# Two interleaved memory-attention layers with gated feed-forward: weights fetched piece by piece, clearing moved to the prologue, one flip and two copies placed elsewhere

## The chip, the cores and the metric

The kernel runs on one core of a Trainium2 chip. Its time is device microseconds of one execution. Five engines work side by side: TensorE (PE in the profile; PEld is its weight load), VectorE (DVE), ScalarE (ACT), GpSimd (POOL) and SyncE (SP), which here issues nearly all DMAs. Each runs its own instructions in a fixed order and waits on semaphores for the others. Matmuls write to PSUM, whose eight banks VectorE or ScalarE must copy out ("evacuate") before they are used again.

## The reference

The input x has 2048 tokens of 448 elements. Two layers follow each other; each adds a memory attention and a gated feed-forward, and both layers use the same weights:

```python
x = x + attention(layernorm(x), mem0, Wq, Wk, Wv, Wo)
x = x + ((gate * (gate > 0)) * up) @ W_down     # gate, up from layernorm(x)
# attention, for 64 segments of 32 tokens, one after the other:
h = concat([mem, xs])                 # 8 memory rows and 32 tokens
scores = (h Wq)(h Wk)^T * scale       # 16 heads of 256; memory rows see
p = softmax(masked scores)            #   everything, tokens see backwards
o = (p (h Wv)) Wo                     # summed over the heads
mem = o[:8]; out = o[8:]
```

A segment needs the memory rows that the one before it left, so the 64 segments of a layer are a chain.

## The kernel before, in words

**Prologue** (L222 to L372). For each of eight pairs of heads the kernel loads Wq and Wk, turns them on TensorE and multiplies them into one matrix A_sb (with A3 and A3z for the last 64 rows of the 448); then Wv and Wo become B_sb. A segment then needs only h A, the scores, the weighted sum of h, and the product with B_sb. The products leave PSUM on VectorE and ScalarE. GpSimd sets up ident, the masks and the token buffers hT, and later clears TQ and xa (L341); after that it is idle until the loop begins.

**The loop** is `step(g, ff)` for g from 0 to 68, written out in full. Chain 0 is layer 1 on segment g, chain 1 is layer 2 on segment g - 4. Steps 4 to 63 have both chains (80 columns: two times 32 tokens and 8 memory rows); steps 0 to 3 and 64 to 67 have one (40 columns). In odd steps from the third on, a `Feed` object does the feed-forward of 128 rows in the gaps. The 16 heads are two halves (`hf`) of 28 tiles of 128 rows. A step goes:

- `pairs`, `wide`, `leave_bank`, `close_bank`: h A for the tiles of each half, into PSUM banks named b0 to b3 and z0 for half 0, c0 to c3 and z1 for half 1 (`prj` in the profile). `leave_bank` copies a bank into TQ, or TZ for the last 64 dimensions, the queries of that half.
- `scores_m`, `scores_x`: scores of the memory rows (`Sm`) and the tokens (`Sx`), then the softmax over VectorE (maximum mx, difference se, sum ssum, reciprocal rs, product) and ScalarE (exponential), into PM and PX.
- `flipped`, `flipped_rows`: PM or PX turned on TensorE into `pps` and copied out as PT.
- `weigh_m`, `weigh_m_rows`, `weigh_x`: the weighted sums of hk (the turned h). `weigh_m` makes two PSUM tiles, ya (tiles 0 to 15, 256 columns) and yb (tiles 16 to 27, 192 columns), and copies them into the memory columns of Y or Z (L711, L716). Y and Z are two buffers per half, 28 tiles x 80 columns, used in turns from step to step; token columns are filled by `weigh_x` a step ahead.
- `project_out`, `project_tail`: Y or Z times B_sb into `ox` (the first 384 output dimensions) and `o` (the last 64), over columns lo to hi; `finish` writes the new memory rows into hT for the next step and the outputs into OT. In step 0 the only outputs are eight memory columns, 32 to 40.

**Order.** On TensorE it is the order of the source: each matmul or turn is tied to the one before it (`in_order`, L73). On the other engines a scheduler orders the instructions by when it expects them to be ready, so the copy of one score can stand ahead of another that the source names first. A few are pinned (`keep_in_program_order`).

**Buffers.** The pool `glob` lasts for the whole kernel. The prologue's pool `pre` is closed at its end, and the pool `main` then takes its memory, so what is written first in `main` waits for the last use of `pre`. In `main` lie the feed-forward weights Wgu_sb and Wd_sb, and Y, Z, TZ, PX, PM, OT, hk and hh, which are cleared there (L404 to L419), Y, Z and hh by GpSimd, the others by VectorE; GpSimd also copies eight blocks of ident into TZ (L408).

**Feed-forward weights.** `load_ff(part)` (L381) issues up and gate rows (two DMAs of 224 KB) for parts 0 to 6, and 256 rows of Wd (one DMA) for parts 7 to 13. `load_some` issues two parts: at three places in steps 0 and 1, at two in step 2. Each DMA waits for the TensorE instruction that stands last in the source at that place.

Of the kernel before, what the change touches and what calls it, by code (L numbers as in the profile page):

```python
# [8 lines left out]
BF = mybir.dt.bfloat16  # L9
# [11 lines left out]
SEG = 32  # L21
L = MEM + SEG
F = 1792
FT = 14
# [6 lines left out]
NT = 28  # L31
HI = 128
HW = 5 * HI
W = 2 * L
XO = (0, 2 * L - SEG)
M0 = SEG
HX = (0, 64 + MEM)
HM = (SEG, 64)
QR = (64, 96)
NPASS = 7  # L40
ROWS = (slice(0, 64), slice(64, 128))


def chunk_of(i, r):

    return 6 if i == 3 else 2 * i + r if i < 3 else 2 * (i - 4) + 1 - r
# [7 lines left out]
def build_kernel(ctx, tc, A_x, A_mem0, A_Wq, A_Wk, A_Wv, A_Wo, B_W_gate, B_W_up, B_W_down, out,  # L54
                 ntiles=16, nseg=64):
    nc = tc.nc
    P = nc.NUM_PARTITIONS
# [9 lines left out]
    glob = ctx.enter_context(tc.tile_pool(name="glob", bufs=1))  # L67
# [19 lines left out]
    def behind_pe(r):  # L87
        tc.add_manual_dep(r.ins, last_pe[0],
                          mybir.DependencyInfo(mybir.DependencyClass.Sync, mybir.DependencyReason.DATA),
                          reason="order of work")  # L90
# [7 lines left out]
    xa = [glob.tile([P, DM], BF, name=f"xa{i}") for i in range(3)]  # L98
# [7 lines left out]
    ident = glob.tile([P, P], BF, name="ident")  # L106
# [49 lines left out]
    TQ = []  # L156
    for hf in range(2):
        t = glob.tile([P, 5, 6, 64], BF, name=f"TQ{hf}")
        TQ.append(t)

    def flip_banks():

# [59 lines left out]
    with tc.tile_pool(name="pre", bufs=3) as pre:  # L222
# [115 lines left out]
        idle(32)  # L338
        cur = flip_next(0)
        idle(16)  # L340
        for t in TQ + xa:  # L341
            behind_pe(nc.gpsimd.memset(t[:], 0.0))
        for p in range(NP):
            if p > 1:
                nxt = flip_next(p + 1)
            for _ in fuse_qk_parts(p, cur):
                if p < 2:
                    nxt = flip_next(p + 1)
            cur = nxt
            if p == 2:  # L350
                xn0 = normed(st0)
            if p == 4:
                tps0 = transpose_tokens(xn0)
                for b in range(2):
                    rows_in(nc.vector, b, 0, tps0[:, :, block(b)])
                mtp = psum.tile([P, 4, MEM], BF, tag="ps", name="mtp")
                for kd in range(4):
                    tr(mtp[:, kd, :], mem0_n[:, kd * 128:(kd + 1) * 128], ident[0:MEM, 0:MEM])
                nc.vector.tensor_copy(mem0T[:], mtp[:])
                set_mem(0, mem0T[:].unsqueeze(2), (0,))  # L360
# [17 lines left out]
    Wgu_sb = main.tile([P, NPASS, F], BF, name="Wgu_sb")  # L378
    Wd_sb = main.tile([P, FT, DM], BF, name="Wd_sb")

    def load_ff(part):  # L381

        def piece(dst, src):
            d = nc.sync.dma_start(dst, src)
            tc.add_manual_dep(d.ins, last_pe[0],
                              mybir.DependencyInfo(mybir.DependencyClass.Sync, mybir.DependencyReason.DATA),
                              reason="order of transfers")

        if part < NPASS:
            for r, src in enumerate((B_W_up, B_W_gate)):  # L390
                c = chunk_of(part, r)
                piece(Wgu_sb[ROWS[r], part, :], src[64 * c:64 * c + 64])
        else:
            f = slice(2 * (part - NPASS), 2 * (part - NPASS) + 2)
            piece(Wd_sb[:, f, :], B_W_down[f.start * P:f.stop * P].rearrange("(f p) d -> p f d", p=P))

    TZ, PX, PM = [], [], []
    YY = [[], []]
    swap = main.tile([P, W], F32, name="swap")
    for hf in range(2):  # L400
        for name, shape, where in (("Y", [P, NT, W], YY[hf]), ("Z", [P, NT, W], YY[hf]), ("TZ", [P, 5, 128], TZ),
                                   ("PX", [P, 4, 64], PX), ("PM", [P, 2, 64], PM)):
            t = main.tile(shape, BF, name=f"{name}{hf}")
            (nc.gpsimd if name in "YZ" else nc.vector).memset(t[:], 0.0)  # L404
            where.append(t)
        for part, q in enumerate(QR):
            for c in range(2):
                nc.gpsimd.tensor_copy(TZ[hf][q:q + 16, 3 * c + part, :].rearrange("p (h q) -> p h q", q=16),  # L408
                                      ident[q:q + 16, q:q + 16].unsqueeze(1).to_broadcast([16, 8, 16]))
    OT = main.tile([P, 4, 128], BF, name="OT")  # L410
    nc.vector.memset(OT[:], 0.0)
    xT = main.tile([P, NPASS, 128], BF, name="xT")
    hh = main.tile([P, FT, 128], BF, name="hh")
    part = main.tile([P, 2, DM], F32, name="part")
    nc.gpsimd.memset(hh[:], 0.0)
    HK = []
    for i in range(2):
        t = main.tile([P, 6, 128], BF, name=f"hk{i}")
        nc.vector.memset(t[:], 0.0)  # L419
        HK.append(t)  # L420


    class Feed:
# [133 lines left out]
    def wide(bk, chains, hb, j, tiles=slice(0, 6)):  # L557

        n = L * len(chains)
        for t in bk.tiles[tiles]:  # L560
            for kd in range(3):
                mm(bk.out(t, n), A_sb[:, kd, bk.hf, t, :], moving(hb, j, kd, chains),
                   start=(bk.empty and kd == 0 and t == bk.tiles[0]), stop=(not bk.empty and kd == 2),
                   skip_group_check=True)
        bk.empty = False
# [28 lines left out]
    def close_bank(bk, chains, hb, j, eng, **how):  # L594

        wide(bk, chains, hb, j)
        leave_bank(bk, chains, eng, **how)
# [49 lines left out]
    def active(g):  # L647
        return [c for c in (0, 1) if 0 <= g - c * LAG < nseg]

    at = [0]  # L650

    def step(g, ff):
        chains = active(g)
        xs = active(g - 1)
# [2 lines left out]
        hb = hTb[gb % 2]  # L657
        cols = [(0, 32) if c == 0 else (48, 80) for c in xs] + [(32, 40) if c == 0 else (40, 48) for c in ms]
        lo, hi = min(a for a, _ in cols), max(b for _, b in cols)
        last = g == nseg + LAG - 1  # L660
        now = 0 if chains else 1
        if not chains:
# [8 lines left out]
        def ys(hf, later=0):  # L671
            return YY[hf][(g + later) % 2]

# [28 lines left out]
        def probs_x(hf, Sp):  # L702
            weights_of(Sp, 4, PX[hf], f"x{hf}")

        def weigh_m(hf, hk, PT):
            if not ms:
                return
            ya = psum.tile([P, 256], F32, tag="ps", name="ya")
            for kd in range(2):
                mm(ya[:, kd * 128:kd * 128 + 128], hk[:, kd, :], PT[:], start=True, stop=True)  # L710
            nc.vector.tensor_copy(ys(hf)[:, 0:16, M0:M0 + 16], ya[:].rearrange("p (t q) -> p t q", q=16))  # L711
            yb = psum.tile([P, 192], F32, tag="ps", name="yb")
            mm(yb[:, 0:128], hk[:, 2, :], PT[:], start=True, stop=True)
            for eo in range(2):
                mm(yb[:, 128:192], hk[:, 4 + eo, :], PT[:, 64 * eo:64 * eo + 64], start=(eo == 0), stop=(eo == 1))
            nc.scalar.copy(ys(hf)[:, 16:28, M0:M0 + 16], yb[:].rearrange("p (t q) -> p t q", q=16))  # L716

        def weigh_m_rows(hf, hk, PT):
            pt = PT[:, 0:128].rearrange("p (t c m) -> p t c m", c=2, m=MEM)
# [49 lines left out]
        def project_out(hf, t0, t1):  # L769

            nonlocal ox
            if ox is None:
                ox = psum.tile([P, 3, W], F32, tag="ox", bufs=1, name="ox")
            for t in range(t0, t1):
                for mc in range(3):
                    mm(ox[:, mc, lo:hi], B_sb[:, hf, t, mc * 128:(mc + 1) * 128],
                       ys(hf, now)[:, t, lo:hi], start=(hf == 0 and t == 0 and mc == 0),
                       stop=(hf == 1 and t == NT - 1 and mc == 2), skip_group_check=True)
# [31 lines left out]
                for u in us:  # L810
                    ff.gate_up(u)

        def load_some():
            if g < 3:
                for part in (2 * at[0], 2 * at[0] + 1):
                    if part < NPASS + FT // 2:
                        load_ff(part)
                at[0] += 1

        if not chains:  # L820
            project_tail()
            project_out(0, 0, NT)
# [1 line left out]
            finish()  # L824
            return

        load_some()
        nc.gpsimd.tensor_copy(hb[ROWS[0], j, 4 * HI:4 * HI + 104], hb[ROWS[0], j, 3 * HI:3 * HI + 104])
        b0, b2 = Bank(0, 0), Bank(0, 2)
        pairs((b0, b2), chains, hb, j)  # L830
# [7 lines left out]
            ff.residual()  # L838
            ff.norm(nc.gpsimd if len(chains) == 2 else None)
        hk = hk_make(kps)  # L840
        load_some()
        b1, z0 = Bank(0, 1), Bank(0, 4)
        wide(b1, chains, hb, j)
        wide(z0, chains, hb, j)
# [6 lines left out]
        pairs((c0, c2, c1, c3), chains, hb, j)  # L851
        close_bank(b3, chains, hb, j, nc.vector, parts=(slice(2, 3), slice(0, 2), slice(3, 5)))
        close_bank(z1, chains, hb, j, nc.scalar)
        wide(c0, chains, hb, j, slice(0, 1))
        scores_m(0)
        wide(c0, chains, hb, j, slice(1, 6))
# [2 lines left out]
        close_bank(c1, chains, hb, j, nc.scalar if len(chains) == 2 else nc.vector)  # L859
        if ff is not None and len(chains) == 1:  # L860
            tps = ff.xposed()
        if len(chains) == 2:
            pm = flipped(PM[0], 1, "m0", own)
        close_bank(c3, chains, hb, j, nc.scalar, parts=(slice(0, 3), slice(3, 5)))
        if ff is not None and len(chains) == 1:
            ff.xposed_rest(tps)
        if len(chains) == 2:
# [14 lines left out]
        if last:  # L882
# [9 lines left out]
            ff.down()  # L892
            ff.leave()
            return
        if g < 2:
            load_some()
        if ff is not None:
            project_out(0, 0, 10)
            half1 = weights_begin(Sx1, 4, PX[1], "x1")
# [18 lines left out]
            weigh_x(1, hk, px1)  # L918
            return
        project_out(0, 0, 23)  # L920
        probs_x(1, Sx1)
        pm = flipped(PM[1], 1, "m1")
        px0 = flipped(PX[0], 2, "x0")
# [1 line left out]
        weigh_m_rows(1, hk, pm)  # L925
        weigh_x(0, hk, px0)
        project_tail()
        project_out(1, 0, 16)
        px1 = flipped(PX[1], 2, "x1")
        project_out(1, 16, NT)  # L930
        finish()
# [84 lines left out]
```

## Time and profile before

| | |
|---|---|
| median of three runs | 1559.07 us (1558.81 to 1559.97) |
| profiled execution, its own time | 1563.11 us |
| its span in the profile | 1561.2 us |
| PE busy | 1534.6 us (98%) |
| DVE, ACT, POOL busy | 1062.3, 805.3, 167.6 us |
| chain that ended last | PE 94%, DVE 3%, ACT 1%, issue 1%, POOL 1%, DMA 1% |
| prologue ends, step 0 begins on PE | 71.4 us |
| steps 1, 2, 3 begin on PE | 90.0, 106.8, 122.8 us |
| an even and an odd two-chain step | 17.7 and 26.4 us |

A line of a timeline gives start, duration, engine, source line, operation, output <- inputs, shape and count; neighbours of one kind are merged into one line, and in brackets stand the idle time before and what ended it. A line of the waits names who waited for whom, the microseconds in total, how often, and the longest. "issue" is a wait for nothing that the profile shows. PE's rows can be busy while its instructions are slow: the granted clock stands apart.

### The profile page before, as it was taken

Reading aid. Unit: us, or ns where it says so; the run is one execution under the profiler, and the core shown is the slowest. Engines: PE = TensorE matmul, PEld = TensorE weight load, DVE = VectorE, ACT = ScalarE, POOL = GpSimd, SP = SyncE. Lnnn points to the kernel's source line nnn. Section 1 sums busy time; section 2 is a strip of 40 time slices with the busy share of each in tenths; the row PEclk is TensorE's granted clock in tenths of the full one; section 3 lists DMA queues with packets and bytes.
Section 4 is the critical chain, followed back from the end, with each engine's and each line's share of the span. In section 5 each row is a group of like instructions: output and inputs, shape, how many; then the busy total and the mean of one; then the engine's idle time right before and its main releaser. Section 6 shows DMA issues by size and latency. Waiting matters only on the chain.

```text
span 1561.2 us, 97869 instructions
## 1 busy us (share of the span) xinstructions
PE 1534.6 (98%) x44947; PEld 1416.4 (91%) x44947; DVE 1062.3 (68%) x3810; ACT 805.3 (52%) x2378; POOL 167.6 (11%) x303
## 2 busy tenths in 40 slices
PE   9889999999999999999999999999999999999998
PEld 7588999999999999999999999999999999999987
DVE  6756766766667666666666667766676767667664
ACT  6634555555455545555455455554555455554443
POOL 3110111011001110111011110110011110110100
PEclk9989999999999999999999999999999999999998
DMA  9530000000000000000000000000000000000000
GB/s 280 144 96 9 9 10 8 6 9 10 10 10 10 10 10 5 9 10 10 10 10 10 10 8 6 10 10 10 10 10 10 10 7 7 10 9 7 7 7 6
DMA packets 29467, 33.10 MB, mean 21 GB/s; under 512 B 3320, under 2 KB 28160, under 8 KB 29056
## 3 DMA queue, kind: packets, MB, share of 16 engines
q1 hardware_dynamic: 28848, 26.74, 6.4%
q8 instruction: 351, 5.75, 1.5%
q14 instruction: 60, 0.49, 0.1%
q10 hardware_dynamic: 144, 0.11, 0.1%
q0 software_dynamic: 64, 0.01, 0.0%
HBM read 23.18 MB, written 1.84 MB: 16 GB/s over the span
## 4 chain that ended last, share of the span: by engine, by line
PE 94%; DVE 3%; ACT 1%; issue 1%; POOL 1%; DMA 1%; SPq 0%; POOLq 0%; ACTq 0%; DVEq 0%
PE prj L82 29%; PE ox L82 25%; PE ups L82 10%; PE dps L82 6%; PE o L82 5%; PE y L82 4%; PE Sx L82 3%; PE pps L85 1%; PE aps L82 1%; PE Sm L82 1%; PE bps L82 1%; PE tps L85 1%; PE gps L82 1%; PE flip L85 1%; PE tpw L85 1%
## 5 line engine op out<-in xcount | busy, mean ns | idle before, releaser
L82 PEld LDWEIGHTS <-B_sb 128*128 128x128 bf16 (+1 forms) x15232 | 492.7, 103 | 26.3 <-issue 18.2
L82 PE MATMUL prj<-hT,A_sb 128*128 128x80 bf16 (+1 forms) x11424 | 436.7, 200 | 0.9 <-issue 0.9
L82 PEld LDWEIGHTS <-A_sb 128*128 128x128 bf16 x11424 | 411.3, 100 | 8.6 <-issue 1.0
L82 PE MATMUL ox<-Y,B_sb 128*128 128x80 bf16 (+3 forms) x5712 | 218.5, 199 | 0.6 <-DVE Y L711 0.6
L82 PE MATMUL ox<-Z,B_sb 128*128 128x80 bf16 (+2 forms) x5712 | 218.3, 200 | 0.6 <-DVE Z L711 0.6
L82 PE MATMUL ups<-xT,Wgu_sb 64*128 64x128 bf16 (+1 forms) x3332 | 190.3, 213 | 2.1 <-DVE hh L469 1.3
L82 PE MATMUL gps<-xT,Wgu_sb 64*128 64x128 bf16 (+1 forms) x3332 | 190.1, 213 | 0.4 <-DVE Z L95 0.4
L94 ACT CAST TQ<-prj 128x480 bf16<-128x480 f32 (+3 forms) x424 | 176.2, 461 | 25.1 <-PE prj L82 22.6
L82 PEld LDWEIGHTS <-Wgu_sb 64*128 64x128 bf16 x6664 | 178.5, 94 | 5.3 <-issue 3.1
L95 DVE CAST TQ<-prj 128x192 bf16<-128x192 f32 (+3 forms) x364 | 139.2, 418 | 63.1 <-PE prj L82 63.1
L94 ACT CAST Z<-y 64x128 bf16<-64x128 f32 (+2 forms) x260 | 89.5, 371 | 141.9 <-PE y L82 85.7
L94 ACT CAST TZ<-prj 64x320 bf16<-64x320 f32 (+2 forms) x304 | 111.8, 378 | 79.6 <-PE prj L82 74.8
L468 ACT CAST ut<-ups 128x256 bf16<-128x256 f32 (+1 forms) x238 | 85.2, 359 | 79.1 <-PE gps L82 59.8
L469 DVE SCALAR_TENSOR_TENSOR hh<-gps,ut 128x256 bf16<-128x256 f32 (+1 forms) x238 | 94.0, 406 | 47.0 <-ACT ut L468 34.2
L94 ACT CAST Y<-y 128x512 bf16<-128x512 f32 (+1 forms) x252 | 87.5, 375 | 62.0 <-DVE Y L95 58.8
L94 ACT COPY hT<-tps 128x256 bf16<-128x256 bf16 x32 | 11.9, 372 | 192.6 <-DVE hT L95 192.6
L95 DVE CAST Z<-y 64x128 bf16<-64x128 f32 (+2 forms) x260 | 103.6, 420 | 9.0 <-ACT Z L94 4.6
L95 DVE CAST Y<-y 128x512 bf16<-128x512 f32 (+1 forms) x252 | 102.6, 418 | 9.0 <-ACT Y L94 3.7
L611 ACT ACTIVATE se<-se 128x80 f32<-128x80 f32 (+1 forms) x270 | 71.5, 298 | 48.2 <-DVE se L610 46.7
L617 DVE TENSOR_REDUCE ssum<-se 128x2 f32<-128x80 f32 (+1 forms) x270 | 70.4, 275 | 37.6 <-ACT se L611 36.8
L82 PE MATMUL dps<-Wd_sb,hh 128*128 128x448 bf16 (+1 forms) x476 | 92.0, 360 | 0.0
L180 POOL TENSOR_SCALAR rstd<-mv 128x1 f32<-128x1 f32 x67 | 15.2, 226 | 715.5 <-DVE mv L178 715.4
(133 smaller groups left out, 2227.2 us busy)
## 6 DMA issues: line engine op xcount, KB each, us to landing
wo<-in_A_Wo_dram SPq DMA_DIRECT2D x8, 448.0 KB, 6.1
nat<-in_A_Wq_dram SPq DMA_DIRECT2D x8, 384.0 KB, 6.1
nat<-in_A_Wk_dram SPq DMA_DIRECT2D x8, 384.0 KB, 6.1
nat<-in_A_Wv_dram SPq DMA_DIRECT2D x8, 384.0 KB, 6.7
xa<-in_A_x_dram SPq DMA_DIRECT2D x32, 56.0 KB, 2.3
xa<-xp SPq DMA_DIRECT2D x32, 56.0 KB, 1.9
out_dram<-xa SPq DMA_DIRECT2D x32, 56.0 KB, 2.0
xp<-in_A_x_dram SPq DMA_DIRECT2D x30, 56.0 KB, 2.2
```

The source lines that it names most:

```text
L82: in_order(nc.tensor.matmul(*a, **k))
L85: in_order(nc.tensor.transpose(*a))
L94: return nc.scalar.copy(dst, src)
L95: return eng.tensor_copy(dst, src)
L180: nc.gpsimd.tensor_scalar(out=rstd[:], in0=mv[:, 1:2], scalar1=EPS, scalar2=None, op0=ALU.add)
L468: nc.scalar.copy(ut[:, :, n], ups[:, :, n])
L469: nc.vector.scalar_tensor_tensor(out=hh[:, 2 * u:2 * u + 2, n], in0=gps[:, :, n], scalar=0.0, in1=ut[:, :, n], op0=ALU.max, op1=ALU.mult)
L611: nc.scalar.activation(se[:], se[:], AF.Exp, scale=SCALE)
L617: nc.vector.tensor_reduce(ssum[:], se[:], axis=AX.X, op=ALU.add)
```

## The change

- **Weights.** The DMAs become a list of 21 pieces of 224 KB: up and gate rows in turns, then Wd. `load_piece` issues one. It is called at the start of each step, behind hk, ahead of the first scores and behind the second, and in steps without `Feed` also at three places among the projections: seven a step in steps 0 to 2.
- **Buffers.** TZ, PX, PM, OT and hk lie in `glob` and are cleared on GpSimd in the prologue, behind TQ and xa; TZ's blocks of ident are copied there too. Of Y and Z, only the 32 token columns of the two Y are cleared; the rest and hh no longer are.
- **Step 0** projects columns 0 to 40 in place of 32 to 40.
- **Flip.** In two-chain steps the flip of PM of half 0 stands behind the first two of the six tiles of bank c3, not ahead of the bank.
- **Copies.** ya leaves PSUM on ScalarE and yb on VectorE, the other way round from before.

```diff
+    TZ, PX, PM = ([glob.tile(shape, BF, name=f"{name}{hf}") for hf in range(2)]
+                  for name, shape in (("TZ", [P, 5, 128]), ("PX", [P, 4, 64]), ("PM", [P, 2, 64])))
+    OT = glob.tile([P, 4, 128], BF, name="OT")
+    HK = [glob.tile([P, 6, 128], BF, name=f"hk{i}") for i in range(2)]
...
-        for t in TQ + xa:
+        for t in TQ + xa + TZ + HK + PM + PX + [OT]:
             behind_pe(nc.gpsimd.memset(t[:], 0.0))
+        for hf in range(2):
+            for part, q in enumerate(QR):
+                for c in range(2):
+                    nc.gpsimd.tensor_copy(TZ[hf][q:q + 16, 3 * c + part, :].rearrange("p (h q) -> p h q", q=16),
+                                          ident[q:q + 16, q:q + 16].unsqueeze(1).to_broadcast([16, 8, 16]))
...
+    pieces = [(Wgu_sb[ROWS[r], part, :], src[64 * chunk_of(part, r):64 * chunk_of(part, r) + 64])
+              for part in range(NPASS) for r, src in enumerate((B_W_up, B_W_gate))]
+    pieces += [(Wd_sb[:, f:f + 2, :], B_W_down[f * P:(f + 2) * P].rearrange("(f p) d -> p f d", p=P))
+               for f in range(0, FT, 2)]
+
+    def load_piece():
+        if pieces:
+            d = nc.sync.dma_start(*pieces.pop(0))
             tc.add_manual_dep(d.ins, last_pe[0],
...
+    YY = [[main.tile([P, NT, W], BF, name=f"{name}{hf}") for name in "YZ"] for hf in range(2)]
     for hf in range(2):
...
+        nc.gpsimd.memset(YY[hf][0][:, :, 0:SEG], 0.0)
...
+        if g == 0:
+            lo = 0
...
-            nc.vector.tensor_copy(ys(hf)[:, 0:16, M0:M0 + 16], ya[:].rearrange("p (t q) -> p t q", q=16))
+            nc.scalar.copy(ys(hf)[:, 0:16, M0:M0 + 16], ya[:].rearrange("p (t q) -> p t q", q=16))
...
-            nc.scalar.copy(ys(hf)[:, 16:28, M0:M0 + 16], yb[:].rearrange("p (t q) -> p t q", q=16))
+            nc.vector.tensor_copy(ys(hf)[:, 16:28, M0:M0 + 16], yb[:].rearrange("p (t q) -> p t q", q=16))
...
+        wide(c3, chains, hb, j, slice(0, 2))
         if len(chains) == 2:
             pm = flipped(PM[0], 1, "m0", own)
-        close_bank(c3, chains, hb, j, nc.scalar, parts=(slice(0, 3), slice(3, 5)))
+        wide(c3, chains, hb, j, slice(2, 6))
+        leave_bank(c3, chains, nc.scalar, parts=(slice(0, 3), slice(3, 5)))
...
         project_out(0, 0, 23)
+        load_piece()
...
         project_tail()
+        load_piece()
         project_out(1, 0, 16)
+        load_piece()
         px1 = flipped(PX[1], 2, "x1")
```

More of the change, by code (lines that the diff above doesn't have):

```diff
@@ L379, in build_kernel @@
     Wd_sb = main.tile([P, FT, DM], BF, name="Wd_sb")
-    def load_ff(part):
-        def piece(dst, src):
-            d = nc.sync.dma_start(dst, src)
+    pieces = [(Wgu_sb[ROWS[r], part, :], src[64 * chunk_of(part, r):64 * chunk_of(part, r) + 64])
[5 more added lines that the diff above has]
+            d = nc.sync.dma_start(*pieces.pop(0))
             tc.add_manual_dep(d.ins, last_pe[0],
@@ L387, in piece @@
                               reason="order of transfers")
[L389 to L398, printed above, removed]
     swap = main.tile([P, W], F32, name="swap")
+    YY = [[main.tile([P, NT, W], BF, name=f"{name}{hf}") for name in "YZ"] for hf in range(2)]
     for hf in range(2):
[L401 to L411, printed above, removed]
+        nc.gpsimd.memset(YY[hf][0][:, :, 0:SEG], 0.0)
     xT = main.tile([P, NPASS, 128], BF, name="xT")
@@ L414, in build_kernel @@
     part = main.tile([P, 2, DM], F32, name="part")
[L415 to L420, printed above, removed]
     class Feed:
@@ L648, in active @@
         return [c for c in (0, 1) if 0 <= g - c * LAG < nseg]
-    at = [0]
     def step(g, ff):
@@ L811, in feed @@
                     ff.gate_up(u)
[L813 to L818, printed above, removed]
         if not chains:
@@ L825, in step @@
             return
-        load_some()
+        load_piece()
         nc.gpsimd.tensor_copy(hb[ROWS[0], j, 4 * HI:4 * HI + 104], hb[ROWS[0], j, 3 * HI:3 * HI + 104])
@@ L840, in step @@
         hk = hk_make(kps)
-        load_some()
+        load_piece()
         b1, z0 = Bank(0, 1), Bank(0, 4)
@@ L894, in step @@
             return
-        if g < 2:
-            load_some()
+        load_piece()
         if ff is not None:
@@ L920, in step @@
         project_out(0, 0, 23)
+        load_piece()
         probs_x(1, Sx1)
@@ L927, in step @@
         project_tail()
+        load_piece()
         project_out(1, 0, 16)
+        load_piece()
         px1 = flipped(PX[1], 2, "x1")
```

## The prediction

> **What bounds the kernel now.** I read the page's head first, then the list of waits of PE by stage, then one-microsecond stretches, then the timeline of single steps. The page:
>
> ```profile
> span 1561.2 us, 97869 instructions
> PE 1534.6 (98%) x44947; PEld 1416.4 (91%) x44947; DVE 1062.3 (68%) x3810; ACT 805.3 (52%) x2378; POOL 167.6 (11%) x303
> PEclk9989999999999999999999999999999999999998
> ```
>
> PE is busy for 98% of the span, and the clock dips in the third slice (78 to 117 us) and in the last one. So there are two places to gain: the few stalls of the start, and gaps too short for a list of waits that come back in each of the 60 two-chain steps. The waits of PE, first from 71 to 181 us (steps 0 to 5), then from 181 to 1475 us:
>
> ```profile
> PE prj L82 <- DVE hk L95: 1.5, 2, 1.0
> PE Sx L82 <- POOL TZ L408: 1.1, 1, 1.1
> PE prj L82 <- issue: 0.9, 1, 0.9
> PE Sx L82 <- issue: 0.6, 1, 0.6
> ...
> PE ya L82 <- DVE PT L630: 0.2, 1, 0.2
> ```
>
> In the first stage PE waits for clearing work (hk, TZ) and twice for "issue", which is nothing the profile names; in the long middle it waits once, for 0.2 us. The stretches of the first step (columns: busy time of PE, PEld, DVE, ACT, POOL, granted clock, DMA share, GB/s):
>
> ```profile
> 79.00:80.00 1.00, 0.56 (x11) 0.41 (x8) 1.00 (x6) 0.26 (x2) 1.00 (x1) 1.00 1.06 242
> 80.00:81.00 1.00, 0.09 (x3) 0.10 (x3) 0.62 (x4) 0.46 (x3) 0.94 (x3) 1.00 0.54 116
> 81.00:82.00 1.00, 0.35 (x10) 0.25 (x10) 0.00 (x0) 0.00 (x0) 0.90 (x4) 0.88 0.06 22
> 88.00:89.00 1.00, 1.00 (x38) 1.00 (x35) 0.00 (x1) 0.00 (x0) 0.26 (x1) 0.50 0.00 0
> 96.00:97.00 1.00, 1.00 (x47) 1.00 (x44) 0.30 (x3) 0.97 (x7) 0.00 (x0) 1.00 0.92 267
> ```
>
> PE nearly stops at 80 to 82 us, the clock halves, and it stays halved through stretches in which PE is busy all the time (88 to 89, the 8-column projection) until after 95 us. Now an even and an odd two-chain step:
>
> ```profile
> 412.07 1.99 PE L82 MATMUL prj<-hT,A_sb 128*128 128x80 bf16 x51
> 413.91 0.23 PE L85 MATMUL pps<-ident,PM 128*128 128x128 bf16 x1
> 414.82 0.62 ACT L94 CAST TQ<-prj 128x288 bf16<-128x288 f32 x2 [0.16 <-PE prj L82]
> 415.46 0.41 DVE L711 CAST Y<-ya 128x256 bf16<-128x256 f32 x1
> 415.81 0.18 PE L82 MATMUL Sx<-hT,TZ 128*128 128x40 bf16 x1
> 415.93 2.63 PE L82 MATMUL ox<-Y,B_sb 128*128 128x80 bf16 x69
> ...
> 429.97 1.99 PE L82 MATMUL prj<-hT,A_sb 128*128 128x80 bf16 x51
> 431.57 0.33 DVE L620 TENSOR_TENSOR PM<-se,rs 128x80 bf16<-128x80 f32 x1
> 431.96 0.23 PE L85 MATMUL pps<-ident,PM 128*128 128x128 bf16 x1
> 434.04 0.18 PE L82 MATMUL Sx<-hT,TZ 128*128 128x40 bf16 x1
> 434.06 1.24 PE L82 MATMUL ox<-Z,B_sb 128*128 128x80 bf16 x30
> ```
>
> The same 51 matmuls (36 ns each) lead to the flip of PM (pps) in 1.84 us in the even step and in 1.99 us in the odd one, where PM is written until 431.90. And from the last Sx matmul to the first ox it is 0.12 us in the even step, 0.02 in the odd: in the even one ox waits for the copy of ya, done at 415.87.
>
> **The change, part by part.**
>
> Flip inside the last bank. Six of c3's eighteen matmuls now go ahead of the flip: 6 x 0.036 = 0.215 us more for PM. In the odd step PE would come to the flip at 431.96 - 0.15 + 0.215 = 432.02, and PM let it start at 431.96 already: the wait goes, with 0.06 us to spare. I read 0.15 to 0.16 us in 29 odd steps (210 to 1448 us), 0.07 in the first, and some 0.01 in each of 30 even ones: 4.6 + 0.07 + 0.3 = 4.95 us. What is late next: PT, 0.27 us behind the flip and 0.22 long, is done at 432.5, and ya is due at 432.91: 0.4 us of cover. c3 itself ends no later than before, since the flip is only moved within it. Bounds: 0 (the wait comes back at ya) and 5.0.
>
> ya on ScalarE, yb on VectorE. In the even step ScalarE is held by the evacuation of c3 until 414.82 + 0.62 = 415.44; ya is then ready. Nothing in this trace copies 128x256 of ya on ScalarE; the nearest row is the copy of ups, 128x256 in 0.37 us (yb's 128x192 takes 0.32). So 415.44 + 0.37 = 415.81 in place of 415.87: 0.06 us, times 30 even steps 1.8 us. Bounds: the whole gap, 0.093 x 30 = 2.8, and a loss if the copy is placed behind another ScalarE instruction (an exponential, 0.28 us: 30 x 0.2 = 6 us lost); I take 1.8, for the copy of yb starts at 415.45 today, in the very place. VectorE's copy gets shorter (192 for 256 columns, some 0.06 us), so the softmax behind it is not later. In six one-chain steps (1 to 3, 64 to 66) ox starts 0.39 us behind the last Sx, 0.35 of it a wait; there ScalarE is idle, and the copy ends some 0.15 us earlier, but VectorE's softmax bounds the next flip, and it gains only the 0.06 to 0.1 us of the shorter copy: 0.1 x 6 = 0.6 us (0 to 2.1). Behind the new wait stand, on ScalarE, the exponentials of the same step; they start at 416.29, 0.4 us after ya is out.
>
> Clearing in the prologue. It takes 2.2 us of VectorE (72.15 to 74.33) and from GpSimd two Z and most of Y (1.96 us each; 32 of 80 columns remain, about 0.8 us each) off the start of step 0, and moves TZ's eight copies. PE's wait for hk (0.99 us at 73.9) and for TZ (1.12 us at 79.8) go: 2.1 us. The price: 3.6 us of memsets (0.87 ns an element, from 1.96 us for 2240) and 2.2 us of copies on GpSimd behind the 1.30 us of xa, some 14.8 to 20.6 us. GpSimd has nothing else to do until 71.46, and VectorE's casts of A_sb take 0.51 us beside today's GpSimd memsets (10.55) and without them (20.30): price 0, and if VectorE were held by all of it, 5.8 us.
>
> Forty columns, and the clock. The 0.5 clock lasts from 81.8 to 95.4 us. Step 2 is the same work as step 1 at full clock. By first matmuls, steps 0, 1 and 2 take 18.65 (71.38 to 90.03), 16.73 and 16.08 us, and step 2 without its 0.90 us of "issue" 15.18. So step 0 loses 3.47: 2.1 by clearing, 1.06 by "issue" (0.65 and 0.41), some 0.3 by the clock; step 1 loses 1.55 by the clock. With no stop of 1.1 us in step 0, I take it that the clock stays: 1.85 us. The wider projection costs nothing at full clock (69 matmuls over 40 columns 1.89 us in step 1, over 8 columns at half clock 1.99 in step 0); at half clock 36 ns for 28, x224, 1.8 us.
>
> [...]
>
> Weights in pieces. 21 transfers of 224 KB, seven a step in steps 0 to 2, in place of groups of four and of seven behind each other. No transfer is added, and SP has none queued behind them until step 3. The last is asked for in step 2 before its final twelve tiles (near 121 us today) and takes 4.3 us; step 3 first needs up and gate weights at 133. "Issue" takes 0.65, 0.41 and 0.90 us while or just after weights move, but also 0.49 at 138 us, where none do. I take 1.5 of 1.96 us; bounds 0 and 1.96.
>
> [...]
>
> Sum: 4.95 + 1.8 + 0.6 + 2.1 + 1.85 + 1.5 = 12.8 us. The profiled execution took 1563.11 us (span 1561.2), 4.04 above the median of 1559.07; I take the gain off both: 1550.3 profiled, 1546.3 median.
>
> **The rivals.**
>
> A. The start only moves its stalls: "issue" stays (1.5 back), and step 0 still falls to half clock (1.85 back, and up to 1.8 for the wider columns at that clock): 1549.6 to 1551.4, say 1550. For it: the half clock came after two stalls, and step 0 keeps waits of 0.2 us each for PT. Against: steps 1 and 2 have those too at full clock.
>
> B. Two-chain steps gain nothing: what PE saves at the flip it waits at ya or ox. 1546.3 + 6.75 = 1553. Against: 0.4 us of cover at ya.
>
> C. The tail loses its half clock, 6.8 us from 1535.8, whose fourteen dps matmuls would take 0.19 for 0.37 us each: 2.6 us less, 1543.7. It stands in one window of low PE use, whose place shifts with 12.8 us.
>
> D. Slower. The order on ScalarE comes out so that ya's copy stands behind an exponential or a second evacuation in every two-chain step. It decides from a start 0.22 us later (12.8 / 60); at 0.3 us it takes all back and 5 us more: 1564. For it: engines run their copies in an order fixed beforehand, which every edit may change. Against: ya is ready first and needed first.
>
> **How the numbers follow.** Forecast 57% (own range 1544.5 to 1549), A 15%, B 9%, C 12%, D 5%, no change 2%. The range 1542 to 1553.5 leaves out D, no change, half of B's spread and the low end of C's; its ends are B and C with 0.5 to 1.7 us more. A difference below 0.2% (3.1 us) can't be told from none; faster by more 0.93, within 0.02, slower 0.05.
>
> **What would show it.** Right: no PE wait for TZ or hk in step 0, granted clock 1.00 from 71 to 130 us, step 0 near 15.3 us; 57 prj matmuls ahead of pps and no 0.15 us gap in odd steps; ya's copy on ScalarE done before the last Sx; pairs of steps in 43.95 us for 44.18. Wrong: a new wait of ya for PT, ox for yb, VectorE slower from 15 to 21 us, "issue" above 0.4 us, or a half clock in step 0.

## The result and the profile after

The changed kernel took 1546.27 us, the median of four runs (1544.2 to 1548.19), beside 1559.52 for the kernel before: a ratio of 0.9915, 95% interval 0.9897 to 0.9932, 13.25 us faster. The forecast was 1546.3. Two repeats, each beside further runs of the kernel before, gave 12.25 and 11.0 us less, so 13.25 is the largest of three readings. The profiled execution took 1544.2 us, the shortest of its four, while the profiled one of before, 1563.11, was longer than the four behind the median of 1559.52; so I don't read the change from the difference of the two spans, but from stages.

The page's head of the changed kernel:

```profile
span 1542.4 us, 97875 instructions
PE 1519.4 (99%) x44947; PEld 1406.8 (91%) x44947; DVE 1056.7 (69%) x3801; ACT 804.9 (52%) x2378; POOL 163.6 (11%) x309
PEclk9999999999999999999999999999999999999999
```

PE has the same 44947 instructions and 15 us less busy time, and no slice shows a low clock. The waits of PE from 70 to 175 us:

```profile
PE prj L82 <- issue: 1.3, 2, 0.9
PE o L82 <- issue: 1.1, 1, 1.1
...
PE ya L82 <- DVE PT L618: 0.9, 4, 0.2
...
PE prj L82 <- DVE hk L95: 0.4, 1, 0.4
```

The wait for TZ is gone and that for hk is down to 0.4 us, outside step 0. "Issue" is still there, 2.4 us of it. In the profile before there were 2.0 us by the same list from 70 to 140 us: the waits of 0.9 and 0.6 us that the prediction shows, and one more:

```profile
PE o L82 <- issue: 0.5, 1, 0.5
```

An even and an odd two-chain step of the changed kernel:

```profile
403.12 2.21 PE L82 MATMUL prj<-hT,A_sb 128*128 128x80 bf16 x57
405.17 0.22 PE L85 MATMUL pps<-ident,PM 128*128 128x128 bf16 x1
...
404.18 2.29 ACT L94 CAST TQ<-prj 128x480 bf16<-128x480 f32 x5
...
406.06 0.27 PE L82 MATMUL ya<-PT,hk 128*128 128x128 bf16 x2
406.37 0.38 ACT L699 CAST Y<-ya 128x256 bf16<-128x256 f32 x1
...
406.84 0.18 PE L82 MATMUL Sx<-hT,TZ 128*128 128x40 bf16 x1
406.87 2.63 PE L82 MATMUL ox<-Y,B_sb 128*128 128x80 bf16 x69
...
420.90 2.21 PE L82 MATMUL prj<-hT,A_sb 128*128 128x80 bf16 x57
422.95 0.22 PE L85 MATMUL pps<-ident,PM 128*128 128x128 bf16 x1
```

57 matmuls now lead to the flip, in 2.05 us in both steps: the odd step no longer waits for PM. From the last Sx to the first ox it is 0.03 us where it was 0.12, because ScalarE's copy of ya is done at 406.75.

The stages, cut at the first prj matmul of each step, in three profiles of the changed kernel (the second and third are the repeats):

| us | before | changed | second | third |
|---|---|---|---|---|
| prologue | 71.38 | 70.11 | 72.53 | 71.38 |
| step 0 | 18.65 | 14.19 | 14.19 | 14.19 |
| steps 1 to 3 | 55.66 | 54.14 | 56.16 | 57.34 |
| two-chain steps 4 to 63 | 1321.66 | 1313.35 | 1313.64 | 1313.44 |
| steps 64 to 66 | 55.80 | 55.16 | 55.39 | 55.38 |
| step 67 and tail | 38.11 | 35.45 | 38.68 | 36.85 |

The two-chain steps give 8.2 us in all three, step 0 gives 4.46, steps 64 to 66 give 0.5, and steps 1 to 3 give, on the mean, nothing (55.9): step 1 alone takes 16.1 us for 16.7, but step 3 23.9 for 22.9. That is 12.9 us. Prologue and tail vary by 2 to 3 us between executions of the same kernel, and of the kernel before there is one profile only.

### The profile page after: what moved, and what is told of

Read it like the earlier page. It is cut to its first block, busy times and chain, and to the rows that moved or that the text cites. A ratio compares the mean times of both kernels' runs of the same rounds, so it can differ in the third digit from the quotient of the medians.

```text
span 1542.4 us, 97875 instructions
## 1 busy us (share of the span) xinstructions
PE 1519.4 (99%) x44947; PEld 1406.8 (91%) x44947; DVE 1056.7 (69%) x3801; ACT 804.9 (52%) x2378; POOL 163.6 (11%) x309
## 3 DMA queue, kind: packets, MB, share of 16 engines
q8 instruction: 351, 5.75, 1.6%
## 4 chain that ended last, share of the span: by engine, by line
PE 94%; DVE 2%; DMA 1%; ACT 1%; issue 1%; SPq 0%; POOL 0%; POOLq 0%; ACTq 0%; DVEq 0%
PE prj L82 30%; PE ox L82 25%; PE ups L82 10%; PE dps L82 6%; PE o L82 5%; PE y L82 4%; PE Sx L82 3%; PE Sm L82 1%; PE bps L82 1%; PE pps L85 1%; PE gps L82 1%; PE tps L85 1%; PE aps L82 1%; PE flip L85 1%; DMA nat<-in_A_Wk_dram 1%; PE ym L82 1%
## 5 line engine op out<-in xcount | busy, mean ns | idle before, releaser
L82 PE MATMUL ox<-Y,B_sb 128*128 128x80 bf16 (+2 forms) x5712 | 218.2, 199 | 0.3
L457 DVE SCALAR_TENSOR_TENSOR hh<-gps,ut 128x256 bf16<-128x256 f32 (+1 forms) x238 | 94.1, 406 | 46.8 <-ACT ut L456 33.9
```

The source lines that it names most:

```text
L82: in_order(nc.tensor.matmul(*a, **k))
L457: nc.vector.scalar_tensor_tensor(out=hh[:, 2 * u:2 * u + 2, n], in0=gps[:, :, n], scalar=0.0, in1=ut[:, :, n], op0=ALU.max, op1=ALU.mult)
```

## The experiments

Kernels of one group ran on one chip and share the runs of the kernel before: e1 to e4 (1559.4); the repeat r0, e5 to e7 (1561.03); e8 and e9 (1561.14); r1 and r2 (1561.3). All edits are against the changed kernel, but for e9. The theory at the outset was the prediction's own: flip and copies carry the two-chain steps, clearing and the clock the start, and the weights' traffic causes "issue". Against it stood that "issue" has another cause, and that the clock depends on more than PE's stalls.

**The flip undone**

```diff
-        wide(c3, chains, hb, j, slice(0, 2))
         if len(chains) == 2:
             pm = flipped(PM[0], 1, "m0", own)
-        wide(c3, chains, hb, j, slice(2, 6))
-        leave_bank(c3, chains, nc.scalar, parts=(slice(0, 3), slice(3, 5)))
+        close_bank(c3, chains, hb, j, nc.scalar, parts=(slice(0, 3), slice(3, 5)))
```

> The changed kernel with the flip of PM back ahead of bank c3. By the prediction's sum this gives back 4.95 us (0.15 to 0.16 us in 29 odd two-chain steps, 0.01 in the even ones): odd steps 26.43 us in place of 26.27, even ones 17.65 in place of 17.64, the run near 1551. The rival (what PE saves at the flip it would wait for anyhow at ya) expects odd steps of 26.27 and no change.

Measured: 1553.5 us, ratio 0.9961 (0.9945 to 0.9977). An odd step takes 26.435 us as before (26.270 changed), an even one 17.658 (17.637); the two-chain stage is 6.2 us longer than in the changed kernel. The odd step of this kernel:

```profile
426.88 1.99 PE L82 MATMUL prj<-hT,A_sb 128*128 128x80 bf16 x51
428.86 0.23 PE L85 MATMUL pps<-ident,PM 128*128 128x128 bf16 x1
```

51 matmuls and then 0.15 us of waiting for PM, as before the change. The flip's place is worth 29 x 0.165 + 30 x 0.02 = 5.4 us in the steps that repeat. The rest of the 6.2 us is "issue": one wait of 1.1 us at 175 us, which in the three profiles of the changed kernel is 0, 0.4 and 0.4 us. The run came out 2.5 us above the 1551 that was expected.

**The copies exchanged back**

```diff
-            nc.scalar.copy(ys(hf)[:, 0:16, M0:M0 + 16], ya[:].rearrange("p (t q) -> p t q", q=16))
+            nc.vector.tensor_copy(ys(hf)[:, 0:16, M0:M0 + 16], ya[:].rearrange("p (t q) -> p t q", q=16))
...
-            nc.vector.tensor_copy(ys(hf)[:, 16:28, M0:M0 + 16], yb[:].rearrange("p (t q) -> p t q", q=16))
+            nc.scalar.copy(ys(hf)[:, 16:28, M0:M0 + 16], yb[:].rearrange("p (t q) -> p t q", q=16))
```

> The changed kernel with ya copied on VectorE and yb on ScalarE again. The prediction's sum gives 1.8 us for the 30 even steps (0.06 each) and 0.6 for six one-chain steps: 2.4 back. The trace of the changed kernel says more: no gap at all is left ahead of ox in even steps (25 ns from the last Sx to the first ox, 118 before), so 0.093 x 30 = 2.8 us, and in one-chain steps ox starts 0.13 us sooner: 2.8 + 0.8 = 3.6 back, even steps 17.74 us.

Measured: 1550.91 us, 0.9944 (0.9929 to 0.9959). Even steps take 17.731 us, odd ones 26.269. The even step:

```profile
411.16 0.18 PE L82 MATMUL Sx<-hT,TZ 128*128 128x40 bf16 x1
411.27 2.63 PE L82 MATMUL ox<-Y,B_sb 128*128 128x80 bf16 x69
```

The gap of 0.11 us before ox is back. The copies are worth 30 x 0.094 = 2.8 us there and 0.76 in the six one-chain steps, whose gap went from 387 to 261 ns. Step 0 has the same copies: it takes 14.75 us for 14.19, with waits for Y (0.21 us) and PT (0.24 and 0.17) that are under 0.1 us in the changed kernel. The 2.8 us and the flip's 5.4 are the 8.2 us of the two-chain steps.

**Eight columns in step 0**

```diff
-        if g == 0:
-            lo = 0
```

> The changed kernel with step 0 projecting columns 32 to 40 again. If stalls of PE alone bring the clock down (as the prediction has it), nothing changes: step 0 at 14.2 us and granted clock 1.00 through 71 to 110 us. [...]

Measured: 1547.0 us, 0.9916 (0.9895 to 0.9938), not to be told from the changed kernel by time. Step 0 is 15.08 us for 14.19, and the clock tells more. The projection of step 0 in the changed kernel, then in this one, each from the timeline of PE:

```profile
77.64 1.90 PE L82 MATMUL ox<-Y,B_sb 128*128 128x40 bf16 x69
```

```profile
77.61 1.87 PE L82 MATMUL ox<-Y,B_sb 128*128 128x8 bf16 x69
```

The same instructions at the same time, of 40 columns and of 8. Stretches of the changed kernel (length, busy time of PE, PEld, DVE, ACT, POOL, granted clock, DMA share, GB/s), then of this one:

```profile
78.00:79.00 1.00, 1.00 (x47) 1.00 (x43) 1.00 (x8) 0.00 (x0) 0.00 (x0) 1.00 0.38 56
81.00:82.00 1.00, 1.00 (x62) 0.97 (x59) 0.35 (x2) 0.64 (x3) 0.00 (x0) 1.00 0.56 183
```

```profile
78.00:79.00 1.00, 1.00 (x47) 1.00 (x44) 1.00 (x8) 0.00 (x0) 0.00 (x0) 1.00 0.28 32
80.00:81.00 1.00, 1.00 (x17) 0.56 (x17) 0.79 (x5) 0.70 (x2) 0.00 (x0) 0.69 0.37 68
83.00:84.00 1.00, 1.00 (x37) 1.00 (x35) 0.08 (x1) 0.00 (x0) 0.27 (x1) 0.50 0.41 57
91.00:92.00 1.00, 1.00 (x47) 1.00 (x44) 0.45 (x2) 0.95 (x6) 0.00 (x0) 1.00 0.06 15
```

With 8 columns the clock falls at 80.38 us and stays at half for 10.24 us, although PE had only one stall of 0.23 us in the 4 us before and its rows are busy 0.92 to 1.00 of each microsecond from 77 us on. Narrow matmuls kept PE's rows busy here and did not hold the clock. This is one profile, and half clock comes at other places in another execution; but in all nine profiles with 40 columns, the clearing in the prologue and the weights not all at once, the clock stays up through step 0. Steps 0 and 1 together take 30.96 us for 29.59 to 30.81 in the changed kernel's three profiles, so the loss is at most 1.4 us.

**Weights in groups of two parts**, at the places of the kernel before

```diff
+    groups = [2] * NPASS + [1] * (FT // 2)
...
+    def load_some():
+        for n in groups[0:2]:
+            groups.pop(0)
+            for _ in range(n):
+                load_one()
...
-        load_piece()
+        if g < 3:
+            load_some()
...
-        load_piece()
+        if g < 2:
+            load_some()
```

`load_one` issues one piece. The first of these places is the step's start, and a second like it stands behind hk; the place with `g < 2` stands behind the second scores. `load_piece` does nothing at the places that are left.

> The changed kernel with the weight transfers issued in groups of two parts again. By the prediction's sum PE's waits called issue in steps 0 to 2 grow by 1.5 us. The rival, formed from the trace of the changed kernel: those waits are PE's own instruction fetch, pages of 256 instructions that come no faster than one in about 3.4 us, while 40-column steps at full clock use one up in about 3.3 us; they come at the same instructions with and without weights, and the sum of issue waits from 70 to 140 us stays at 2.4 to 2.9 us, the run within 0.5 us of the changed kernel's.

Measured: 1549.37 us, 0.9933 (0.9918 to 0.9948). Step 0 is 0.67 us longer than in the changed kernel, steps 1 to 3 are 54.70 us, within the changed kernel's 54.14 to 57.34. "Issue" from 70 to 140 us is 2.9 us; in the three profiles of the changed kernel 2.4, 3.1 and 4.7. So the pieces move the stalls to a later step and do not remove them. By time, groups and pieces are not told apart, since the intervals of the changed kernel's three ratios reach from 0.9897 to 0.9943.

**The changed kernel again, beside the next three**

> The changed kernel as it is, once more, to see how far its own executions differ: 1544 to 1549 us. The half-clock windows of 3.4 us lie differently in each execution, and PE's waits called issue come at the same instructions (some 3400, 4400 and 6200 PE instructions into the run) with other lengths: steps 0 to 3 in 68 to 70.5 us, even and odd two-chain steps at 17.64 and 26.27 us again.

Measured: 1548.78 us, 0.9922 (0.9905 to 0.9939). Steps 0 and 4 to 63 repeat the first profile to 0.3 us. The rest doesn't: half clock for 3.41 us at 108.5 and at 125.6 us and for 6.83 us in the tail.

**Clearing back in the main part**

```diff
-        for t in TQ + xa + TZ + HK + PM + PX + [OT]:
+        for t in TQ + xa:
...
+        for name, shape, where in (("Y", [P, NT, W], YY[hf]), ("Z", [P, NT, W], YY[hf]), ("TZ", [P, 5, 128], TZ),
+                                   ("PX", [P, 4, 64], PX), ("PM", [P, 2, 64], PM)):
+            t = main.tile(shape, BF, name=f"{name}{hf}")
+            (nc.gpsimd if name in "YZ" else nc.vector).memset(t[:], 0.0)
...
+    nc.gpsimd.memset(hh[:], 0.0)
```

The tiles lie in `main` again; OT and hk are cleared and TZ's blocks of ident are copied there too, as in the kernel before.

> The changed kernel with clearing and TZ's copies back at the start of the loop. By the prediction's sum 2.1 us come back in step 0 through PE's waits for hk and TZ, and up to 1.85 more if the clock falls behind them, as it did before; with 40 columns it should be up again after one or two windows of 3.4 us in place of four. So step 0 at 16.3 to 17.2 us, run 1548.5 to 1550.5. If the stalls only moved elsewhere, step 0 stays at 14.2 to 15.1 us.

Measured: 1551.39 us, 0.994 (0.992 to 0.9959), 2.6 us over the changed kernel on the same chip. Step 0 is 16.81 us for 14.19, 2.62 more: the waits for hk (1.0 us) and TZ (0.7) come back, and so does half clock at 75.25 us, for 3.41 us. The prologue is 70.23 us, near the low end of the 70.1 to 73.1 us of the kernels that clear there, so it shows no price of the added GpSimd work, but nothing finer than these 3 us. The casts of A_sb say more: with GpSimd clearing beside them, two in a row take VectorE 1.01 us in the changed kernel, and 1.01 us in this one without.

**All 21 transfers at the first place**

```diff
     def load_piece():
-        if pieces:
+        while pieces:
```

> The changed kernel with all 21 weight transfers issued one behind the other at the start of step 0. If weight traffic holds up PE's instructions (the prediction), the issue waits of steps 1 and 2 (1.3 us in the changed kernel's profile) vanish, since no weights move there any more, and step 0 gets them. If it is the fetch of instructions by itself, they stay at the same instructions, 0.4 us or more in step 1 or 2, and about 1 us in step 3, and the run stays within 1.5 us of the changed kernel.

Measured: 1552.83 us, 0.9943 (0.9926 to 0.996). The run is 4.0 us over the changed kernel on the same chip. Steps 0 to 2 take 50.84 us for 44.88 to 46.89 in the changed kernel's three profiles. The waits of PE from 70 to 125 us and the worst stretch:

```profile
PE flip L85 <- issue: 3.2, 1, 3.2
PE o L82 <- issue: 1.9, 1, 1.9
...
PE prj L82 <- issue: 0.4, 1, 0.4
```

```profile
82.00:83.00 1.00, 0.24 (x16) 0.13 (x10) 0.58 (x2) 0.33 (x2) 0.00 (x0) 1.00 1.03 251
```

While the 4.7 MB move, with the DMA engines full, PE stands for 3.2 and 1.9 us. So this traffic made "issue" long. But when all weights are in, waits of 0.4 us in step 2 and 0.6 in step 3 remain, with nothing moving from 104 to 140 us but eleven packets of instructions. So neither of the two expectations held alone: traffic stretches a shortage that is there without it.

**Long matmuls that nobody reads**, to see whether PE lacks time or instructions

```diff
+        if g in (1, 2):
+            longer = psum.tile([P, 512], F32, tag="ps", name="longer")
+            for _ in range(4):
+                mm(longer[:], ident[:], A_sb[:, 0, 0, 0:4, :], start=True, stop=True)
         load_piece()
```

> The changed kernel with four matmuls of 512 columns more at the start of steps 1 and 2, whose result nobody reads: 0.85 us of PE time in eight instructions. If PE runs short of instructions in these steps, the fetch gains that time, the issue waits there (0.9 and 0.5 us in the changed kernel's profile) shrink by as much, and steps 1 and 2 together grow by 0.7 us or less. If instructions are not what is short, both steps grow by 0.85 us: 1.7 together.

Measured: 1547.03 us, 0.9909 (0.9892 to 0.9925), beside 1548.78 for the changed kernel on the same chip. Eight matmuls of 0.21 us each, 1.7 us of added work, and "issue" from 70 to 140 us is 0.8 us for 3.1; no half clock in steps 1 to 3. The steps 0 to 3 take 67.94 us, no more than the best of the changed kernel's three (68.33 to 71.53). Part of the waiting only comes later: waits of 0.3 and 1.1 us at 168 to 171 us, where the changed kernel has 0 to 0.4. From 70 us to the end "issue" is 3.2 us here, and 3.2, 5.1 and 6.3 in the changed kernel's three profiles.

**More of them**: four at the start of steps 1, 2, 3 and of the last step, and four and two in two gaps of the last step

```diff
+        if g in (1, 2, 3) or last:
+            longer(4)
...
+            longer(4)
             feed(0, 1, 2, 3)
...
             feed(6)
+            longer(2)
```

> The changed kernel with four matmuls of 512 columns at the start of steps 1 to 3 and of the last step (67), four more there ahead of the feed-forward, and two ahead of its last weighted sum, all unread: some 4.7 us of PE time at full clock. If PE is short of instructions in these steps, and if its stalls bring the half-clock windows, the added matmuls fill stalls: steps 0 to 3 at 67 to 68.5 us, no half clock in the tail, the run at 1545 to 1548 and no longer than the changed kernel. If the stalls have another cause, the run is 4 to 5 us longer: 1551 to 1553.

Measured: 1545.29 us, 0.9894 (0.9878 to 0.9909); "issue" 1.6 us from 70 to 140 us; no half clock until the last 0.05 us of the span; step 67 and tail 34.37 us. Steps 0 to 3 take 69.40 us, more than the 67 to 68.5 expected. The first four matmuls of step 67 stand ahead of its first prj matmul and so count to steps 64 to 66, which take 56.81 us for 55.2 to 55.4.

**Forty columns alone, in the kernel before**

```diff
         lo, hi = min(a for a, _ in cols), max(b for _, b in cols)
+        if g == 0:
+            lo = 0
```

> The kernel before with step 0 projecting columns 0 to 40, nothing else. The stalls of step 0 stay (TZ, hk, issue), so the clock still falls near 82 us; with 40 columns it should be back after one or two windows of 3.4 us in place of four: half clock for 3.4 to 6.8 us, steps 0 and 1 together 1 to 1.5 us shorter than 35.4. By the prediction's prices the wider matmuls cost up to 1.8 us as long as the clock is halved, so the run itself comes out within 1.5 us of the kernel before.

Measured: 1561.09 us, 0.9996 (0.9985 to 1.0008): no change. Its stretches from 82 us on:

```profile
82.00:83.00 1.00, 1.00 (x36) 1.00 (x34) 1.00 (x6) 0.09 (x1) 1.00 (x1) 0.50 0.07 16
...
85.00:86.00 1.00, 1.00 (x37) 0.76 (x37) 0.00 (x0) 0.72 (x3) 0.00 (x0) 1.00 0.85 237
```

The clock still falls, since the stalls for hk and TZ are there, but for 3.41 us in place of 13.65. Steps 0 and 1 gain 1.5 us by it in the profile, and "issue" ahead of prj grows from 0.9 to 1.9 us. With step 2 and step 3, steps 0 to 3 gain 1.2 us. The medians show none of it, but their interval, 2.3 us less to 1.2 us more, doesn't exclude it. That the half clock got shorter holds beyond the one profile: the mean granted clock is 0.9963 in the ten runs of this kernel and 0.9929 in the thirteen of the kernel before, which is 10.6 us less at half clock (0.001 of the clock is 3.1 us of it). So these 10 us at half clock were worth 2.3 us at most, the wider matmuls' own cost taken off; 69 matmuls of 8 columns take 1.99 us at half clock in the trace before and 1.87 at full clock in e3.

**Changed kernel and the longer one head to head**

> The changed kernel once more, on the chip of the next run: 1545 to 1549 us, steps 0 to 3 in 68 to 70.5 us, half clock for 3.4 to 6.8 us somewhere in the one-chain steps or the tail in about half of the executions.

> The kernel with the unread long matmuls in steps 1 to 3 and 67 once more, beside the changed kernel: 1 to 3 us shorter than that if the added work keeps the clock up and only fills waits for instructions; equal or longer if its first result was chance.

Measured: the changed kernel 1550.31 us, 0.9923 (0.9903 to 0.9943); with the 22 unread matmuls 1544.77, 0.9888 (0.9863 to 0.9913). The kernel with 4.7 us more work for PE is 5.5 us shorter than the changed one, and shorter than the kernel before. All its four runs (1543.88 to 1545.45) lie below all six of the other (1546.12 to 1553.43), though the two intervals against the kernel before touch. 5.5 us is the largest difference on record: beside the changed kernel's other medians, 1546.27 and 1548.78, this kernel's two are 1.0 to 4.0 us less. The changed kernel came out above its expected 1549 us, and its steps 0 to 3, 71.53 us, above the expected 70.5. Waits from 70 to 140 us, changed and longer:

```profile
PE prj L82 <- issue: 3.2, 2, 1.8
PE o L82 <- issue: 1.1, 1, 1.1
...
PE ups L82 <- issue: 0.3, 1, 0.3
```

```profile
PE o L82 <- issue: 0.7, 1, 0.7
```

And the tail, where the changed kernel of the earlier repeat runs at half clock behind a stretch in which PE is busy a quarter of the time:

```profile
1523.00:1524.00 1.00, 0.25 (x18) 0.25 (x20) 0.12 (x1) 0.00 (x0) 0.00 (x0) 1.00 0.00 0
1527.00:1528.00 1.00, 1.00 (x8) 0.34 (x7) 0.82 (x3) 0.00 (x0) 0.00 (x0) 0.50 0.00 0
```

In both profiles of the longer kernel the tail keeps full clock. From step 64 to the end, all ten matmuls added there included, they take 91.1 and 91.2 us; the changed kernel's three took 90.6, 92.2 and 94.1. The granted clock of its eight runs is 0.999 to 1.000, of the changed kernel's sixteen 0.994 to 1.000. What the tail's matmuls and the start's are worth apart, and the clock and the waits, was not tried.

## Why the prediction was right, and where its terms were not

The time was right, and 12.9 us by stages stands beside a sum of 12.8. But three terms were too small and one was empty, and they cancel: that the sum came out to 0.1 us is luck, as is the median's 0.03 us, with three readings from 11.0 to 13.25. One of the prediction's own signs of being wrong came up, "issue" above 0.4 us.

- **Flip, 4.95 us: right.** 5.4 us measured by undoing it. The 0.4 us of cover at ya held: no new wait. Rival B falls.
- **Copies, 1.8 + 0.6 us: right in kind, too small.** The even steps gave 0.094 us each and not 0.06, 2.8 us in all, the whole gap; the six one-chain steps gave 0.76, and step 0, which the sum left out, 0.56. The step that mis-sized it is "ScalarE is held by the evacuation of c3 until 415.44; 415.44 + 0.37 = 415.81". In the trace after, ScalarE's evacuations run until 404.18 + 2.29 = 406.47 and ya's copy begins at 406.37: a row's end is 0.1 us later than the start of what follows it, so ya is out 0.1 us sooner than worked out, before the last Sx. Rival D falls: no copy stands behind an exponential.
- **Clearing, 2.1 us: right in kind, too small.** Undone, step 0 loses 2.62 us, and part of it is the half clock of 3.41 us that comes with the stalls. No price shows in the prologue, as taken.
- **Step 0 as a whole, "near 15.3 us": too long.** It takes 14.19. The step that failed is the yardstick: step 2 without its "issue" was taken as the floor of step 0. Undoing gives 2.62 for clearing, 0.89 for the columns, 0.67 for the pieces and 0.56 for the copies, together 4.7 for the 4.46 measured, so they overlap a little. The split of step 0's loss was misread as well: the 0.41 us counted as "issue" is a wait of the weight load at 85.69 us, during which PE itself isn't idle.
- **Clock, 1.85 us: it went for a reason that the prediction had only half.** "With no stop of 1.1 us in step 0, I take it that the clock stays" is wrong as a cause: without those stops but with 8 columns it falls all the same, for 10.24 us in e3. In e5 and e9, which have the stalls and 40 columns, it fell too, but for 3.41 us; the change needed both of its parts. Nor did step 1's 1.55 us arrive: it gained 0.65 us on the mean, step 3 lost 1.0, and steps 1 to 3 together gained nothing.
- **Weights, 1.5 us of "issue": wrong, 0.** From 70 to 140 us PE waited 2.0 us before and 2.4, 3.1 and 4.7 us after. The step "I take 1.5 of 1.96" leaned on the weights that move during or just before three of the stalls. All transfers at once did cause stalls, of 3.2 and 1.9 us in e6, but 22 long matmuls made them fewer without a byte less (from 70 us to the end 1.2 and 2.9 us, for 3.2 to 6.3): what runs short is instructions. The counter-evidence was in the prediction, the 0.49 us at 138 us where nothing moves, and I gave it too little weight. This half of rival A came true.
- **Rival C** happens in some executions: of three profiles of the changed kernel one has no half clock in the tail but for its last 0.4 us, one 3.4 us, one 6.8. The time from step 67 on follows, 35.5, 36.9 and 38.7 us.

The stretch that shows the shortage best is in step 1 of the changed kernel, first its timeline, then its windows:

```profile
87.39 0.42 PE L82 MATMUL prj<-hT,A_sb 128*128 128x40 bf16 x10
...
88.69 0.74 PE L82 MATMUL prj<-hT,A_sb 128*128 128x40 bf16 x23 [0.88 <-issue]
```

```profile
88.00:89.00 1.00, 0.31 (x12) 0.31 (x13) 0.00 (x0) 0.00 (x0) 0.00 (x0) 1.00 0.36 129
```

PE stops in the middle of one bank's projection, whose inputs are all there. The page counts 351 packets of instructions, 5.75 MB, for the whole span: 16.4 KB each, and 2 x 44947 instructions of PE over 351 are 256 each. One-chain steps run a pair of weight load and matmul in 25 ns (69 from 77.64 to 79.38 us), so by estimate a packet lasts 128 x 25 ns = 3.2 us; two-chain steps at 36 ns (57 in 2.05 us) use one in 4.6 us. In the fourteen traces no packet starts sooner than 3.2 us behind the one before, and only a handful in each sooner than 3.4.

The traces also tie the waits to these packets. From 70 us on there are 79 waits of PE for "issue" in the fourteen profiles, and each ends 1.2 to 1.6 us after a packet has landed. They come at the same counts of PE instructions (matmuls and weight loads), though not all of them in every execution: up to 180 us always at 256 times the number of that packet plus 180 to 191, as 3518 with the 13th packet, 4540 with the 17th and 6326 with the 24th. Where unread matmuls shift the program, the wait stays at the count and not at the place in the source: at 8884 it is ahead of o in the changed kernel, ahead of y in e7 and ahead of gps in r2. So these waits are for instructions and not for data.

I read it so: one-chain steps at full clock use instructions as fast as they come, any delay is a stall, and a faster clock only brings the stall sooner. The long matmuls agree, each pair of instructions lasting some 0.21 us. That the fetch sets 3.4 us, rather than following PE at it, was not measured by itself.

## What to carry to other kernels

A wait that is too short for a list of waits, but comes in each of sixty steps, was worth more here than all visible stalls (8.2 us of 12.9): compare the same stretch of an even and an odd step and ask what differs. At the start, ask of each "issue" whether PE lacks data or instructions; a few long matmuls put there tell it within one run, by whether the wait keeps its count of instructions or its place in the source. And count a gain in a stage that runs at the pace of something else as zero until that something is named.

## What the runs showed of the hardware

- Every half-clock stretch that ends within its profile lasts 3.41 us or a multiple of it (6.83, 10.24, 13.65), and they lie at other places in another execution of the same kernel. They go with the spread of the runs: of the changed kernel's sixteen, the eight with a mean granted clock of 0.998 or more take 1546.7 us on the mean, the eight with 0.996 or less 1550.7. That the clock alone makes the difference is not shown: the waits may lengthen both, and e4, with 0.995 to 0.997, spreads by 0.8 us only.
- Time in which PE's rows are busy does not by itself keep the clock up: behind 69 matmuls of 8 columns in 1.87 us it fell to 0.50 for 10.24 us (e3), behind 69 of 40 columns in 1.90 us it stayed at 1.00. Nor do 40 columns hold it up through stalls: in e6 it was down for 10.24 us around a wait of 3.2 us. And in the kernel before it was down for 13.65 us, from 81.76 to 95.42 us, though PE's rows are busy 1.00 of each microsecond from 82 us on.
- More work for the engine that bounds the kernel made it shorter: 22 matmuls of 0.21 us, nobody reading them, and 5.5 us less head to head (1.0 to 4.0 against the other medians).
